# The order of every engine's work, written down as tables instead of planned

## The chip, the cores and the metric

The kernel runs on one core of one Trainium2 chip. The metric is the time of one execution in microseconds (us), as the median of several runs. Names of engines: PE is the matrix engine (TensorE), DVE the vector engine, ACT the scalar engine, POOL is GpSimd, and SP only issues transfers (DMAs) here.

## The reference

Two stages. First a gated linear attention, a recurrence over 768 positions for 4 batches and 8 heads of size 48:

```python
for t in range(S):
    state = alpha[:, :, t, :, None] * state + np.einsum('bhd,bhe->bhde', k[:, :, t], v[:, :, t])
    y[:, :, t] = np.einsum('bhd,bhde->bhe', q[:, :, t], state)
```

Its output, laid out as 3072 tokens of 384 values, goes through two layers of a feed-forward network with a squared relu between them:

```python
h = x @ w_in            # 3072 x 384 times 384 x 2048
r = np.maximum(h, 0.0)
g = r * r
return (g @ w_out).astype(np.float32)
```

## The kernel before, in words

The tokens are cut into 12 groups of 256 positions (`g` 0 to 11: three time blocks of four batches each). The recurrence is turned into matrix products within a group: decays are summed as logarithms by a triangular matrix product, a score product is masked, and a state of 48 x 48 per head is carried from one time block of a batch to the next. Then each group runs through the two layers.

The program is a list of operations, each added with a name, the engine or engines that may run it (`alts`), a cost, a priority, and what it reads and writes. For group `g` the names are:

- loads on SP or POOL: `lda`, `ldk`, `ldq`, `ldv` with the group's number (alpha, k, q, v; 384 KB each). Groups rotate over 4 buffers `raw`. A load of group 5 or later also waits for an operation of the group before: alpha for `ln`, k for `ekm`, q and v for `tr0`; and lda waits for the ldq of the group before it. `lda3` waits for `wout0`.
- weights on POOL: `win0`, `win1` (first layer, each half serves four of the eight steps), `wout0`, `wout1` (second layer).
- decays: `pr` (product of two alphas), `ln` and `lm` (logarithms on ACT), `m1`, `m1i`, `m1s` (PE), `ei`, `ea`, `es`, `ec` (exponentials on ACT), `bk`, `aq`, `lb` (products and a difference on DVE or POOL). For group 0 they come in two halves by heads: `ln0_0`, `ln1_0` and so on.
- `ekm`, `eqm` (scaled keys and queries, DVE), `tr` (transposes: on PE with an eviction `et` for groups 0 to 2, as transposing DMAs `tr0`, `tr1` on SP from group 3), `vc` (v cast to bf16), `p` (scores, PE), `mk` (mask, DVE), `kv` (state update alone), `y` (the output of the group; from group 2 on it also updates the state for the next), `sa`, `sc`, `sd` (the state's steps on DVE or POOL), `xe` (eviction), `xt` (transposed output: PE for groups 0 to 3, a DMA on SP from group 4), `xv`.
- layers: `s1_g_u` for u = 0 to 7 (6 matmuls into one of two banks of PSUM), `re` (relu, which frees the bank), `sq` (square of one or two relu tiles), `s2_g_j_s` (4 matmuls each; all of one j add up in the single bank `psO`), `oe` (eviction, which frees that bank), `out` (store, from two buffers `osb`). The last tile's second layer is `s2_11_1_0` and `s2_11_1_1` in other banks.
- set-up: constants without a name (`c1` and so on), and `table`, an explicit load of ACT's function table with logarithm and exponential (lines 480 to 486).

Before it emits anything, the kernel plans: `schedule` (line 159) replays the program with its costs. Whenever an engine is free, it takes from its ready operations the one of lowest priority. Where more than one engine is allowed, the operation goes to the one that would end it first, with a handicap for POOL (`BIAS`). A table `SHIFT` (line 49) moves the priority of some 360 names. The outcome is one fixed list per engine. On the chip each engine runs its list in order and waits at semaphores where an input is not there yet; nothing is chosen at run time. `fill` puts matmuls on zeros into PE's list where the plan has gaps before the first s1, `place` works out which waits are needed, `emit` writes the five lists.

Of the kernel before, what the change touches and what calls it, by code (L numbers as in the profile page):

```python
# [1174 lines left out]
```

## Time and profile before

| | before |
|---|---|
| median of 3 runs | 174.81 us (174.69 to 175.29) |
| the profiled execution's own time | 176.21 us |
| its span (first to last instruction) | 174.5 us |
| PE busy | 169.1 us, 97% of the span |
| DVE, ACT, POOL busy | 121.3, 117.6, 18.8 us |
| granted clock of PE | 1.00 throughout |
| bytes moved by DMA | 33.36 MB, mean 191 GB/s |

A line of a timeline gives the start, the length, the engine, the line of the kernel, the operation, what it writes and reads, the shape, how many instructions were merged, and in brackets the idle time before it with what ended that. PEld is PE's weight load, which runs beside matmuls. Lines of the engine name "SPq" are issues of transfers; a transfer lands later.

### The profile page before, as it was taken

What the parts mean: (1) busy time and instruction counts of PE and PEld (TensorE: products, weight loads), DVE (VectorE), ACT (ScalarE), POOL (GpSimd) and SP (SyncE); (2) the same over time, 40 slices, a digit from 0 to 9 for tenths busy, and PEclk for the clock granted to TensorE, in tenths of its full rate; (3) what the DMA queues carried; (4) which work ended last, traced back from release to release, by engine and by line L of the source; (5) the groups of instructions that cost most, each with busy time, mean ns of one, the idle gap of its engine ahead of it and who ended that gap; (6) DMA issues with size and microseconds to landing.
All of it is one profiled execution on the core that took longest, in us unless ns stands there. A gap on an engine that the chain in (4) does not pass through costs nothing.

```text
span 174.5 us, 5094 instructions
## 1 busy us (share of the span) xinstructions
PE 169.1 (97%) x2237; PEld 130.5 (75%) x2237; DVE 121.3 (70%) x197; ACT 117.6 (67%) x211; POOL 18.8 (11%) x28
## 2 busy tenths in 40 slices
PE   7989999999999999999999999999999999999994
PEld 2556898856886697777788886778788697688773
DVE  5497799797967869866778966868849726322230
ACT  3848698868869569768768757378668564566440
POOL 3159010022102120000100000000200000000000
DMA  5999999979998999798998897999899690040022
GB/s 139 324 297 190 274 303 216 230 208 280 274 229 125 274 235 188 200 222 151 278 212 211 228 196 180 275 201 251 201 214 208 115 196 4 0 135 4 10 80 90
DMA packets 74743, 33.36 MB, mean 191 GB/s; under 512 B 71649, under 2 KB 71905, under 8 KB 74721
## 3 DMA queue, kind: packets, MB, share of 16 engines
q1 hardware_dynamic: 73184, 28.32, 71.4%
q0 software_dynamic: 1536, 4.72, 12.1%
q8 instruction: 17, 0.28, 0.7%
q14 instruction: 6, 0.04, 0.1%
HBM read 25.17 MB, written 4.72 MB: 171 GB/s over the span
## 4 chain that ended last, share of the span: by engine, by line
PE 56%; DMA 26%; ACT 6%; DVE 4%; SPq 3%; POOL 2%; issue 1%
PE psO L1089 22%; PE psWH L1042 22%; DMA raw<-in_v_dram 9%; DMA wout<-in_moe_w_out_dram 8%; DMA raw<-in_alpha_dram 5%; DMA raw<-in_q_dram 5%; SPq L568 3%; PE psO L1143 2%; POOL raw L568 2%; ACT rr L1050 2%; PE psX L843 2%; PE psX L1012 2%; ACT vbf L742 1%; PE psZ L811 1%; PE psX L832 1%; PE psX L940 1%
## 5 line engine op out<-in xcount | busy, mean ns | idle before, releaser
L1042 PE MATMUL psWH<-xt,win 128*128 128x256 bf16 x576 | 73.9, 275 | 0.5 <-ACT rr L1050 0.2
L1042 PEld LDWEIGHTS psWH<-xt,win 128*128 128x128 bf16 x576 | 65.0, 145 | 6.2 <-DVE rr L1052 1.6
L1089 PE MATMUL psO<-wout,gt 128*128 128x384 bf16 x368 | 68.9, 326 | 0.0
L1050 ACT ACTIVATE rr<-psWH 128x512 bf16<-128x512 f32 x83 | 48.9, 596 | 21.5 <-PE psWH L1042 20.0
L1089 PEld LDWEIGHTS psO<-wout,gt 128*128 128x128 bf16 x368 | 34.8, 98 | 18.3 <-DVE gt L1060 0.2
L1060 DVE TENSOR_TENSOR gt<-rr 128x1024 bf16<-128x1024 bf16 (+1 forms) x47 | 28.4, 608 | 25.1 <-ACT rr L1050 24.5
L951 DVE TENSOR_TENSOR pm<-psX,caus 128x1024 bf16<-128x1024 f32 x12 | 14.6, 1220 | 2.4 <-PE psZ L940 2.1
L951 DVE TENSOR_TENSOR pm<-psZ,caus 128x1024 bf16<-128x1024 f32 x12 | 14.6, 1216 | 1.5 <-PE psZ L940 1.4
L1097 ACT ACTIVATE osb<-psO 128x384 f32<-128x384 f32 x19 | 9.3, 489 | 6.8 <-PE psO L1089 6.3
L971 ACT ACTIVATE xbf<-psX 128x768 bf16<-128x768 f32 x12 | 9.7, 806 | 5.0 <-PE psX L832 4.1
L746 DVE TENSOR_TENSOR qks<-raw,eq 128x384 bf16<-128x384 f32 x18 | 10.3, 605 | 3.0 <-DMA raw<-in_q_dram 3.0
L1143 PE MATMUL psO<-zero 128*128 128x512 bf16 (+1 forms) x37 | 10.5, 417 | 1.3 <-DVE zero L489 1.3
L741 POOL CAST vbf<-raw 128x768 bf16<-128x768 f32 x4 | 3.7, 930 | 71.5 <-DMA raw<-in_v_dram 71.5
L1064 ACT ACTIVATE gt<-rr 128x512 bf16<-128x512 bf16 (+1 forms) x13 | 10.8, 828 | 0.4
L751 DVE TENSOR_TENSOR qks<-raw,ek 128x768 bf16<-128x768 f32 x11 | 10.7, 969 | 0.4 <-ACT ek L663 0.3
L1052 DVE TENSOR_SCALAR rr<-psWH 128x512 bf16<-128x512 f32 x13 | 8.9, 687 | 2.0 <-PE psWH L1042 1.6
L742 ACT ACTIVATE vbf<-raw 128x768 bf16<-128x768 f32 x7 | 5.9, 845 | 3.5 <-DMA raw<-in_v_dram 3.5
L717 ACT ACTIVATE la<-raw 128x384 f32<-128x384 f32 x8 | 4.2, 523 | 5.3 <-DMA raw<-in_alpha_dram 5.2
L1143 PEld LDWEIGHTS psO<-zero 128*128 128x128 bf16 x37 | 3.5, 108 | 4.6 <-issue 1.9
L906 DVE TENSOR_TENSOR smd<-psZ,sbd 128x384 bf16<-128x384 f32 x8 | 4.4, 554 | 3.4 <-PE psX L832 3.4
L675 DVE TENSOR_TENSOR prd<-raw 128x384 f32<-128x384 f32 x7 | 4.0, 569 | 2.9 <-DMA raw<-in_alpha_dram 2.9
L678 ACT ACTIVATE lab<-prd 128x384 bf16<-128x384 f32 x10 | 5.2, 520 | 1.1 <-POOL prd L677 0.6
(115 smaller groups left out, 165.9 us busy)
## 6 DMA issues: line engine op xcount, KB each, us to landing
raw<-in_alpha_dram SPq DMA_DIRECT2D x11, 384.0 KB, 4.2
raw<-in_k_dram SPq DMA_DIRECT2D x11, 384.0 KB, 5.1
raw<-in_q_dram SPq DMA_DIRECT2D x11, 384.0 KB, 4.2
raw<-in_v_dram SPq DMA_DIRECT2D x11, 384.0 KB, 4.8
out_dram<-osb SPq DMA_DIRECT2D x11, 384.0 KB, 4.3
win<-in_moe_w_in_dram POOLq DMA_DIRECT2D x2, 768.0 KB, 9.9
wout<-in_moe_w_out_dram POOLq DMA_DIRECT2D x2, 768.0 KB, 15.2
raw<-in_alpha_dram POOLq DMA_DIRECT2D x1, 384.0 KB, 9.7
```

Source lines behind the costliest of these rows:

```text
L746: add("dve", lambda e, j=j, dst=dst: e.tensor_tensor(dst, RAW[r][:, 2, :, j, :].rearrange("p (n x) d -> p n x d", x=2), EQ[la][:, j].rearr ...
L751: add("dve", lambda e, a=a, E=E: e.tensor_tensor(QKS[qs][:, a, :, :, 0:D], RAW[r][:, 1 + a].rearrange("p h j d -> p j h d"), E[la][:].rear ...
L951: add("dve", lambda e, hf=hf, psT=psT: e.tensor_tensor(PM[pm][:, hf].rearrange("p r n j t -> p (r n) (j t)"), psT[:, :, :].rearrange("p r ...
L971: add("act", lambda e: e.activation(XBF[x2][:], psX[:, :, 0:HD], AF.Copy), act_ns(2 * HD), p0 + 6100, reads=[("ps", "X", 0), ("ps", "X", 1 ...
L1042: ins = pe.matmul(psH[hb][:, i * T:(i + 1) * T], WIN[:, kk, hidden(fj)], mov, start=(kk == 0), stop=(kk == KT - 1))
L1050: add("act", lambda e, hb=hb, rr=rr: e.activation(rr, psH[hb], AF.Relu), act_ns(512), pu + 600, reads=[("ps", "H", hb)], writes=[("rr", rb ...
L1052: alts={"dve": (lambda e, hb=hb, rr=rr: e.tensor_scalar(rr, psH[hb], 0.0, None, ALU.max), dve_ns(512))})
L1060: add("dve", lambda e, dst=dst, sq=sq: e.tensor_tensor(dst, sq, sq, ALU.mult), 148 + k * 267, pu + 1200, reads=[("rr", rb, h) for h in ran ...
L1064: "act": (lambda e, dst=dst, sq=sq: e.activation(dst, sq, AF.Square), act_ns(k * 512))})
L1089: ins = pe.matmul(psS, GT[gt][:, fj, j, :], WOUT[:, fj, :], start=(fj * parts % FT == 0), stop=((fj + 1) * parts % FT == 0))
L1097: add("act", lambda e, j=j, psS=psS: e.activation(OSB[ob][:, j], psS, AF.Copy), act_ns(DM), ps_ + 700, reads=[keyS], writes=[("osb", ob, j ...
L1143: pr.fill(lambda n: lambda pe: pe.matmul(psO[:, 0:n], ZERO[:, 0:128], ZERO[:, 0:n], skip_group_check=True), ((512, 216, 420), (256, 109, 2 ...
```

## The change

The planner no longer chooses. For each engine a table `ORDERS` gives the names in the order in which that engine runs them; every operation is fixed to the engine in whose table it stands. `SHIFT`, `BIAS` and `AFFINITY` go. `schedule` still replays the program to get start times for `fill` and `place`, but takes the next operation from the table. One constant of that replay changes (`DMA_LAST` of POOL, 1900 to 1500). The operations themselves, their sizes, buffers and dependencies stay.

Against the lists of before: 45 operations go from ACT to DVE (30 of them `re`, 4 `xe`, 5 `et`), 33 from DVE to ACT (19 `sq`, 10 `re`), 22 from DVE and 6 from ACT to POOL (15 `sq`, 6 `bk`, 3 `vc`, 2 `sd`, `aq2`, `pr11`), and 5 from POOL to ACT or DVE (`vc5`, `vc7`, `vc10`, `pr3`, `sd2`).

The tables of POOL and SP in full, the others where the text speaks of them:

```diff
+ORDERS = {
+    "pe": """
+        m10_0 m11_0 tr00_0 tr10_0 kv0 p0_0 tr01_0 tr11_0 m11 p1_0 y0 xt0 tr0_1 tr1_1 s1_0_1 s1_0_0 p0_1 s1_0_2 m1i2
+        s1_0_3 kv1 s1_0_4 s1_0_5 y1 s1_0_6 s1_0_7 xt1 m1s2 s2_0_0_0 s1_1_0 s1_1_1 s2_0_0_1 s1_1_2 s1_1_3 tr1_2 tr0_2
+        s1_1_5 s1_1_4 p0_2 s2_0_0_2 s2_0_0_3 s1_1_6 m1i3 s1_1_7 s2_0_1_0 s2_0_1_1 kv2 s2_0_1_2 s2_0_1_3 m1s3 y2
...
+        s2_4_1_3 s1_5_5 s1_5_6 s2_5_0_0 s1_5_7 p0_7 s2_5_0_1 s2_5_0_2 s1_6_1 s1_6_0 s2_5_0_3 y7 s1_6_2 s2_5_1_0 m1i9
+        s1_6_3 s2_5_1_1 s1_6_4 s1_6_5 s2_5_1_2 s2_5_1_3 p0_8 s1_6_7 s2_6_0_0 s1_6_6 s2_6_0_1 s1_7_1 s1_7_0 s2_6_0_2
+        s1_7_3 y8 s1_7_2 s1_7_5 m1i10 s2_6_0_3 s1_7_4 s1_7_7 s2_6_1_0 s2_6_1_1 s2_6_1_2 s2_6_1_3 s1_7_6 p0_9 s2_7_0_0
+        s1_8_1 s2_7_0_1 s1_8_0 s1_8_3 s2_7_0_2 y9 s2_7_0_3 s1_8_2 m1i11 s1_8_5 s2_7_1_0 s2_7_1_1 s2_7_1_2 s1_8_4 p0_10
...
+        s2_10_0_1 s1_11_1 s2_10_0_2 s1_11_4 s1_11_3 s2_10_0_3 s1_11_6 s1_11_5 s2_10_1_0 s2_10_1_1 s2_10_1_2 s2_10_1_3
+        s1_11_7 s2_11_0_0 s2_11_0_1 s2_11_0_2 s2_11_0_3 s2_11_1_0 s2_11_1_1
+    """.split(),
+    "act": """
+        ln0_0 ln1_0 ei0_0 ei1_0 ea0_0 ea1_0 ec1_0 table ec0_0 c23 ln1 et11_0 vc1 ei1 ea1 xe0 et0_1 ec1 re0_0 ln2 ei2
...
+        vc8 re6_0 re6_1 oe5_0 ln9 lm9 re6_2 ei9 ea9 re6_4 sq6_3 oe5_1 es9 sq6_5 re6_6 re7_1 re7_0 lm10 ln10 re7_3 xe8
...
+        sq10_3 oe9_1 re10_7 re11_1 re11_3 oe10_0 sq11_6 oe10_1 sq11_5 oe11_0 oe11_10
+    """.split(),
+    "dve": """
+        c19 c8 c9 c10 c11 c12 c13 c16 c1 c17 c3 c18 c5 c6 ekm0_0 ekm1_0 eqm0_0 c7 et00_0 sa0 et10_0 eqm1_0 mk0_0
+        et01_0 c2 mk1_0 sc0 ekm1 eqm1 xv0 et1_1 re0_1 pr2 mk1_1 re0_2 mk0_1 sa1 sc1 re0_5 xe1 xv1 ekm2 eqm2 et1_2
...
+        re11_0 re11_2 sq10_7 re11_4 re11_6 re11_5 re11_7 sq11_7 oe11_11
+    """.split(),
+    "pool": """
+        c14 c15 c20 c21 c22 vc0 win0 lda2 win1 wout0 sd0 ldk2 ldq2 bk2 wout1 sq0_5 aq2 ldv2 sd1 sq0_6 sq0_7 bk3 vc3
+        pr5 sd3 vc4 bk5 sq2_5 sd4 pr6 bk6 sq3_6 vc6 sq5_6 sq6_1 vc9 sq7_3 bk10 sq7_1 pr11 bk11 sq8_3 sq8_5 sq8_6 sq9_3
+        sq11_1 sq11_3
+    """.split(),
+    "sp": """
+        lda0 ldk0 ldq0 ldv0 lda1 ldq1 ldv1 ldk1 lda3 ldq3 ldk3 ldv3 lda4 ldq4 ldk4 ldv4 lda5 tr1_3 tr0_3 ldk5 tr0_4
+        out0_1 tr1_4 ldq5 out1_1 ldv5 lda6 tr0_5 tr1_5 ldk6 ldq6 xt4 ldv6 lda7 ldk7 tr0_6 tr1_6 xt5 ldq7 out2_1 ldv7
+        out3_1 lda8 tr0_7 ldk8 tr1_7 ldq8 xt6 ldv8 lda9 tr0_8 ldk9 tr1_8 ldq9 xt7 ldv9 lda10 ldk10 tr0_9 out4_1 tr1_9
+        ldq10 xt8 ldv10 lda11 out5_1 ldk11 tr1_10 tr0_10 out6_1 xt9 ldq11 ldv11 tr1_11 tr0_11 out7_1 xt10 out8_1 xt11
+        out9_1 out10_1 out11_0 out11_10 out11_11
+    """.split(),
+}
...
-    BIAS = {"pool": 300}
-    DMA_LAST = {"sp": 800, "act": 800, "pool": 1900}
+    DMA_LAST = {"sp": 800, "act": 800, "pool": 1500}
...
-        op = Op(choices, prio + self.SHIFT.get(name, 0), name)
+        op = Op(choices, prio, name or f"c{len(self.ops)}")
...
+        place = {n: (e, k) for e, names in ORDERS.items() for k, n in enumerate(names)}
+        for op in self.ops:
+            e = place[op.name][0]
+            op.alts = {e: op.alts[e]}
...
-                while avail[e] and free[e] <= now + 1e-9:
-                    o = min(avail[e], key=lambda o: (o.prio, o.idx))
...
-                    avail[e].remove(o)
+                while len(order[e]) in avail[e] and free[e] <= now + 1e-9:
+                    o = avail[e].pop(len(order[e]))
```

For comparison, the lists that the planner of before gives POOL, and the start of ACT's and of PE's:

```text
pool: c14 c15 c20 c21 c22 vc0 win0 win1 sd0 lda2 ldk2 ldq2 ldv2 wout0 wout1 sd1 pr3 sd2 vc4 pr5 vc5 pr6 vc7 vc10
act:  table c23 ln0_0 ln1_0 ei0_0 ea0_0 ei1_0 ea1_0 ec1_0 ec0_0 et10_0 et01_0 ln1 et11_0 ei1 ea1 xe0 ec1 vc1 et1_1 re0_0
pe:   m10_0 m11_0 tr00_0 tr10_0 tr01_0 p0_0 kv0 tr11_0 p1_0 m11 y0 tr0_1 xt0 tr1_1 p0_1 s1_0_0 s1_0_1 kv1 s1_0_2 s1_0_3 y1 s1_0_4
sp:   ... lda8 ldk8 tr0_7 tr1_7 out4_1 xt6 ldq8 ldv8 lda9 ldk9 tr0_8 tr1_8 xt7 ldq9 ldv9 out5_1 lda10 ldk10 tr0_9 ...
```

More of the change, by code (lines that the diff above doesn't have):

```diff
@@ L12 @@
 LN_EXP_TABLE_SET = 6
+ORDERS = {
[3 more added lines that the diff above has]
+        s1_1_5 s1_1_4 p0_2 s2_0_0_2 s2_0_0_3 s1_1_6 m1i3 s1_1_7 s2_0_1_0 s2_0_1_1 kv2 s2_0_1_2 s2_0_1_3 m1s3 y2
+        s2_1_0_0 s2_1_0_1 xt2 m1i4 s2_1_0_2 s1_2_1 s2_1_0_3 s1_2_0 s1_2_3 s2_1_1_0 s2_1_1_1 s1_2_2 s1_2_5 m1i5 p0_3
+        s2_1_1_2 s2_1_1_3 s1_2_4 s1_2_7 y3 s1_2_6 s2_2_0_0 xt3 s2_2_0_1 s2_2_0_2 p0_4 s1_3_1 s1_3_0 s2_2_0_3 s1_3_3
+        s1_3_2 s2_2_1_0 s2_2_1_1 s2_2_1_2 y4 s1_3_4 s1_3_5 m1i6 s1_3_6 s2_2_1_3 p0_5 s1_3_7 s2_3_0_0 s2_3_0_1 s2_3_0_2
+        s2_3_0_3 s1_4_0 s1_4_1 s2_3_1_0 s1_4_2 y5 s1_4_3 s1_4_4 s2_3_1_1 m1i7 s2_3_1_2 s1_4_5 s2_3_1_3 s1_4_6 s1_4_7
+        p0_6 s2_4_0_0 s1_5_1 s1_5_0 s2_4_0_1 s2_4_0_2 s1_5_2 s1_5_3 s2_4_0_3 y6 s1_5_4 s2_4_1_0 s2_4_1_1 m1i8 s2_4_1_2
+        s2_4_1_3 s1_5_5 s1_5_6 s2_5_0_0 s1_5_7 p0_7 s2_5_0_1 s2_5_0_2 s1_6_1 s1_6_0 s2_5_0_3 y7 s1_6_2 s2_5_1_0 m1i9
+        s1_6_3 s2_5_1_1 s1_6_4 s1_6_5 s2_5_1_2 s2_5_1_3 p0_8 s1_6_7 s2_6_0_0 s1_6_6 s2_6_0_1 s1_7_1 s1_7_0 s2_6_0_2
+        s1_7_3 y8 s1_7_2 s1_7_5 m1i10 s2_6_0_3 s1_7_4 s1_7_7 s2_6_1_0 s2_6_1_1 s2_6_1_2 s2_6_1_3 s1_7_6 p0_9 s2_7_0_0
+        s1_8_1 s2_7_0_1 s1_8_0 s1_8_3 s2_7_0_2 y9 s2_7_0_3 s1_8_2 m1i11 s1_8_5 s2_7_1_0 s2_7_1_1 s2_7_1_2 s1_8_4 p0_10
+        s1_8_7 s1_8_6 s2_7_1_3 s1_9_1 s1_9_0 s2_8_0_0 s2_8_0_1 s2_8_0_2 s1_9_3 s2_8_0_3 s1_9_2 y10 s2_8_1_0 s2_8_1_1
+        s1_9_4 s1_9_5 s2_8_1_2 s2_8_1_3 s1_9_7 p0_11 s2_9_0_0 s1_9_6 s2_9_0_1 s1_10_1 s1_10_0 y11 s1_10_2 s2_9_0_2
+        s2_9_0_3 s1_10_3 s1_10_4 s2_9_1_0 s1_10_5 s1_10_6 s2_9_1_1 s2_9_1_2 s1_11_0 s2_9_1_3 s1_10_7 s1_11_2 s2_10_0_0
+        s2_10_0_1 s1_11_1 s2_10_0_2 s1_11_4 s1_11_3 s2_10_0_3 s1_11_6 s1_11_5 s2_10_1_0 s2_10_1_1 s2_10_1_2 s2_10_1_3
[3 more added lines that the diff above has]
+        ln0_0 ln1_0 ei0_0 ei1_0 ea0_0 ea1_0 ec1_0 table ec0_0 c23 ln1 et11_0 vc1 ei1 ea1 xe0 et0_1 ec1 re0_0 ln2 ei2
+        re0_3 sq0_1 ea2 re0_4 sq0_3 ec2 re0_6 re0_7 es2 re1_0 re1_1 sq1_1 re1_3 re1_2 sq1_3 re1_5 sq1_5 ln3 oe0_0 ei3
+        vc2 re1_6 ea3 ec3 sq1_6 oe0_1 es3 ln4 xe2 re1_7 ei4 ea4 lm4 ec4 re2_1 oe1_0 re2_0 es4 re2_3 ln5 re2_2 re2_5
+        sq2_3 ei5 lm5 ea5 re2_4 oe1_1 xe3 re2_7 xv3 ec5 sq2_6 es5 sq2_7 re3_1 re3_0 re3_3 vc5 re3_2 sq3_3 lm6 ln6
+        re3_4 sq3_1 ei6 ea6 oe2_1 ec6 re3_7 sq3_7 es6 oe3_0 re4_0 re4_1 xe5 ln7 re4_3 ei7 re4_5 oe3_1 lm7 ea7 re4_7
+        ec7 sq4_5 es7 re5_0 re5_1 sq4_6 vc7 re5_2 oe4_0 ln8 xe6 re5_4 ei8 lm8 ea8 re5_5 sq5_5 es8 re5_7 re5_6 sq5_7
+        vc8 re6_0 re6_1 oe5_0 ln9 lm9 re6_2 ei9 ea9 re6_4 sq6_3 oe5_1 es9 sq6_5 re6_6 re7_1 re7_0 lm10 ln10 re7_3 xe8
+        re7_2 ei10 oe6_0 re7_4 sq7_5 ea10 oe6_1 es10 re7_6 re8_1 vc10 sq7_6 re8_0 ln11 xe9 ei11 sq8_1 ea11 lm11 re8_5
+        re8_4 re8_7 sq8_7 oe7_1 es11 vc11 re9_0 oe8_0 oe8_1 re9_7 re9_6 re10_0 xe11 sq10_1 oe9_0 re10_3 re10_4 re10_6
+        sq10_3 oe9_1 re10_7 re11_1 re11_3 oe10_0 sq11_6 oe10_1 sq11_5 oe11_0 oe11_10
[3 more added lines that the diff above has]
+        et01_0 c2 mk1_0 sc0 ekm1 eqm1 xv0 et1_1 re0_1 pr2 mk1_1 re0_2 mk0_1 sa1 sc1 re0_5 xe1 xv1 ekm2 eqm2 et1_2
+        et0_2 c4 re1_4 pr3 mk1_2 mk0_2 ekm3 sa2 sc2 eqm1_3 pr4 aq3 eqm0_3 sd2 xv2 sq1_7 bk4 sa3 ekm4 lb4 eqm1_4 eqm0_4
+        sc3 mk0_3 mk1_3 sq2_1 sa4 re2_6 sc4 ekm5 lb5 eqm0_5 eqm1_5 oe2_0 mk1_4 mk0_4 sa5 xe4 sc5 re3_5 sq3_5 re3_6
+        ekm6 lb6 eqm1_6 eqm0_6 mk0_5 mk1_5 re4_2 pr7 sa6 sq4_1 re4_4 sc6 sq4_3 bk7 ekm7 sd5 re4_6 lb7 sq4_7 eqm1_7
+        eqm0_7 mk1_6 mk0_6 re5_3 sq5_1 pr8 sq5_3 sa7 sc7 bk8 oe4_1 ekm8 lb8 eqm1_8 eqm0_8 mk1_7 mk0_7 sd7 pr9 xe7
+        re6_3 sa8 bk9 lb9 re6_5 ekm9 re6_7 eqm0_9 eqm1_9 mk1_8 mk0_8 pr10 sq6_6 sq6_7 sa9 re7_5 re7_7 sd6 lb10 eqm1_10
+        ekm10 eqm0_10 mk1_9 mk0_9 re8_3 sq7_7 oe7_0 sa10 re8_2 lb11 ekm11 mk1_10 re8_6 eqm1_11 re9_1 eqm0_11 mk0_10
+        sq9_1 re9_3 re9_2 xe10 sa11 re9_5 re9_4 sq9_5 mk0_11 sq9_7 mk1_11 re10_1 sq9_6 re10_2 re10_5 sq10_5 sq10_6
+        re11_0 re11_2 sq10_7 re11_4 re11_6 re11_5 re11_7 sq11_7 oe11_11
[13 more added lines that the diff above has]
+}
@@ L42 @@
     SBUF_ONLY = ("pr", "bk", "aq", "ekm", "eqm", "sq", "sb", "sd")
-    BIAS = {"pool": 300}
-    DMA_LAST = {"sp": 800, "act": 800, "pool": 1900}
+    DMA_LAST = {"sp": 800, "act": 800, "pool": 1500}
     SWITCH = 95
     HALVED = {"qks": 3, "kqt": 3, "raw": 3, "ek": 3, "eq": 3, "acm": 2, "laf": 2}
-    AFFINITY = 2500
-    SHIFT = {
[55 rows of a table removed]
-    }
     def __init__(self, nc):
@@ L216, in schedule @@
                 push(0.0, "ready", op)
-        avail = {e: [] for e in engines}
+        avail = {e: {} for e in engines}
         order = {e: [] for e in engines}
@@ L231, in schedule @@
                 elif kind == "ready":
-                    best = None
-                    for e, (_, c) in op.alts.items():
-                        t = max(now, free[e]) + c + self.BIAS.get(e, 0)
-                        t += sum(o.alts[e][1] for o in avail[e] if (o.prio, o.idx) < (op.prio, op.idx))
-                        if best is None or t < best[0]:
-                            best = (t, e)
-                    avail[best[1]].append(op)
-            for e in engines:
-                while avail[e] and free[e] <= now + 1e-9:
-                    o = min(avail[e], key=lambda o: (o.prio, o.idx))
-                    if e == "pe" and o.mode[0] != mode:
-                        same = [x for x in avail[e] if x.mode[0] == mode and x.prio <= o.prio + self.AFFINITY]
-                        if same:
-                            o = min(same, key=lambda o: (o.prio, o.idx))
-                    avail[e].remove(o)
+                    e, k = place[op.name]
+                    avail[e][k] = op
+            for e in engines:
+                while len(order[e]) in avail[e] and free[e] <= now + 1e-9:
+                    o = avail[e].pop(len(order[e]))
                     o.eng = e
```

55 rows, old and new, of the table SHIFT are left out of this document.

## The prediction

> **What bounds the kernel now.** First the page's busy lines, to see whether one engine carries the span.
>
> ```profile
> PE 169.1 (97%) x2237; PEld 130.5 (75%) x2237; DVE 121.3 (70%) x197; ACT 117.6 (67%) x211; POOL 18.8 (11%) x28
> DMA  5999999979998999798998897999899690040022
> ```
>
> PE is busy from end to end, so what can be won is not other engines' work but holes in PE's stream. A busy PE can hide holes (a stalled matmul counts as busy), so I put the planner's order of operations beside the timeline of PE and compared starts. A first-layer step (`s1_g_u`, 6 matmuls) issues in 0.66 us, a second-layer step (`s2`, 4) in 0.65, `p` in 0.57, `y` with a state update in 1.05. From the first s1 (`s1_0_0`) at 18.46 to the last matmul group at 171.17 the stream lasts 152.7 us, and steps that lasted longer than their kind's usual time add up to only 2.3: 0.40 at s1_1_1, 0.12 behind m1i3, 0.14 at kv2 and 0.15 at m1s3 (0.81 before 41 us), 0.15 at m1i6, then 0.37 before y5, 0.25 before y7, 0.41 before s1_7_3 and 0.27 before s1_7_4 (1.30). So 2.3 us is all that a reordering behind 18.46 can return.
>
> What makes the late four holes? The timeline of PE (start, length, engine, line, what) and then that of ACT, around the largest:
>
> ```profile
> 114.34 0.88 PE L1042 MATMUL psWH<-xt,win 128*128 128x256 bf16 x6
> 115.41 0.88 PE L1042 MATMUL psWH<-xt,win 128*128 128x256 bf16 x6 [0.19 <-ACT rr L1050]
> ```
>
> ```profile
> 111.35 0.58 ACT L1050 ACTIVATE rr<-psWH 128x512 bf16<-128x512 f32 x1
> 114.34 0.53 ACT L717 ACTIVATE la<-raw 128x384 f32<-128x384 f32 x1 [2.42 <-DMA raw<-in_alpha_dram]
> 114.77 0.58 ACT L1050 ACTIVATE rr<-psWH 128x512 bf16<-128x512 f32 x1
> ```
>
> ACT's in-order queue holds `lm10`, a logarithm whose load lands at 114.3, ahead of `re7_1`, whose bank PE wants back. ACT idles 2.42 us and PE loses 0.41 + 0.27. The holes before y5 and y7 wait for `vc6` and `vc8` (73.31, 98.62), each started when its v load landed. The chain of waits over 83 to 100 us shows what the loads wait for:
>
> ```profile
> 84.31 4.31 DMA raw<-in_alpha_dram
> ...
> 89.76 0.70 ACT xbf L971
> ...
> 92.86 0.40 SPq L992
> 93.26 0.04 issue
> 93.31 0.58 SPq L568
> 93.89 0.04 issue
> 93.93 4.67 DMA raw<-in_v_dram
> 98.60 0.02 issue
> 98.62 0.85 ACT vbf L742
> ```
>
> Load, logarithm, transpose, then SP's queue, then the next load: a loop of one turn per group. The transpose issue tr0_7 starts at 86.82 and lands 6.2 us later behind two loads, tr0_8 starts at 98.78: 12.0 us a turn, against 12.5 of PE work per group (8 x 0.66 + 8 x 0.65 + p, y, m1i, switches). No slack worth the name: loads, not engine work, make the late holes.
>
> The last view is SP's waits and the head of the loads:
>
> ```profile
> SPq L568 <- DMA wout<-in_moe_w_out_dram: 21.4, 1, 21.4
> ```
>
> lda3, gated on wout0, waits until 30.42, because wout0 is the seventh of the eight POOL transfers (issued at 16.73).
>
> **The change part by part.** Which engine does what moves: by counting names, 28 operations come to POOL and 5 leave it, 45 go from ACT to DVE (30 of them relus), 33 from DVE to ACT. With the means of the rows (relu 0.60 ACT, 0.68 DVE; square 1.06 and 0.69; cast 0.84; reorder of a transpose 1.02 and 0.68) ACT loses about 5.6 us of its 117.6, DVE 2.3 of 121.3. Neither was the bound; beside PE this is worth nothing by itself.
>
> POOL's 28 are the new thing: 15 squares, 6 `bk`, 3 `vc`, 2 `sd`, `aq2`, `pr11`. No square ran on POOL before. Bounds: 0.69 us as on DVE; by its nearest row (`sd`, 384 elements, 0.83 us unhindered) 2.2 us for 1024 elements and 1.1 for 512. POOL is that row's engine, so I take 2.2 and 1.1: 10 x 2.2 + 5 x 1.1 + 13 x 0.85, less 5 x 0.95 = about 34 us more, 53 in all, which fits in 174. What it does to DVE is the question; here POOL's timeline and then DVE's:
>
> ```profile
> 7.93 0.82 POOL L613 CAST vbf<-raw 128x768 bf16<-128x768 f32 x1 [4.98 <-DMA raw<-in_v_dram]
> ```
>
> ```profile
> 7.95 1.21 DVE L620 TENSOR_TENSOR qks<-raw,ek 128x384 bf16<-128x384 f32 x1
> 9.09 0.55 DVE L620 TENSOR_TENSOR qks<-raw,eq 128x384 bf16<-128x384 f32 x1
> ```
>
> The same product takes 0.55 alone and 1.21 when it starts beside a POOL cast: it ends 0.41 after POOL does (8.75). So too the square at 22.56 (1.36 instead of 0.69) beside `sd1`. The Trainium skill ("SBUF — State Buffer", Who interferes with whom) says that a DVE instruction with two SBUF inputs and a GpSimd one that reads SBUF exclude each other, whichever starts first; these rows agree, and the rule speaks against this change. I take +0.2 for PE in the forecast, since most squares sit several PE steps ahead of their `s2`; bounds 0 and the rival's price below.
>
> Head: the new PE order starts s1_0_1 and s1_0_0 before p0_1. win0 lands at 17.9 (issue 9.37 + 8.5), so s1 cannot start before that; it starts 0.5 earlier and p0_1 (0.57) follows: nothing won. DVE now also does et10_0, et01_0 and two memsets (0.42 + 0.42 + 0.38) before xv0, which ended at 16.59 after 1.16 of idle gaps: 16.6 to 17.8, still under win0. But lda2 goes between win0 and win1. Loads in that queue land 1.1 to 1.9 apart (q2 25.8, v2 26.9), so win1 lands at some 22.9 instead of 21.6. By its steps PE reaches s1_0_4 at 17.95 + 4 x 0.72 + 0.57 + 0.27 + 0.45 = 22.1, with y1 (0.8) still to do, and waits 0.7. Part of it returns since m1i2 is already done: +0.4, bounds 0 and +0.85.
>
> wout0 moves ahead of ldk2, ldq2, wout1 and ldv2: a2, win1, wout0 land at about 19.1, 22.9 and 26.4 (3.5 us per weight half, from 26.9 to 30.4), so lda3 starts 4 us sooner. ldv2 now sits behind bk2, wout1, sq0_5 and aq2 on POOL; its issue comes at about 29 instead of 15.9 and lands by 34, while kv2 comes at 36 to 38: hidden, with 2 us to spare. Early holes are rearranged with this: of 0.81 I take half back, -0.4, bounds -0.81 and 0.
>
> Middle: SP's table puts one load ahead of tr0 where two stood (lda6 tr0_5, lda8 tr0_7, lda9 tr0_8), ldq ahead of xt, and stores later (out4_1 behind tr0_9, out5_1 behind lda11). A load's data take 1.2 us of the queue, so a turn of the loop falls from 12.0 to about 10.8, under PE's 12.5. ACT's table puts re7_1 and re7_0 ahead of lm10; vc6 moves to POOL. All four late holes have their cause moved: -1.30, bounds -1.30 and 0. The cost at out4_1: oe6_0 waits for it (two osb buffers), and stores took 1.5 to 6.2 us to land; between tr0_9 and the s2_6_1_0 that needs oe6_0 there are some 7 us of PE work, enough for the median of 3.7.
>
> Tail: after s2_10_1_3 come s1_11_7 and s2_11; sq11_5 (1.06 on ACT) sits behind oe10_1 but has 2 us before s2_11_0_2; sq11_7 has 1.95 us for 0.68 + 0.42. From 171.17 to the end nothing changes.
>
> Sum: -1.30 - 0.4 + 0.4 + 0.2 = -1.1. The profiled execution took 176.21 with a span of 174.5; the median of the runs is 174.81, 0.3 over the span. So a span near 173.4 and a median near 173.7.
>
> **Rivals.**
> The lock decides (slower). A relu ends at 144.16 (started 143.56) and its bank's next s1 starts at 144.67, 0.5 to spare, 0.43 for a DVE relu. Twenty more relus stand in DVE's queue, behind operations with two SBUF inputs that a POOL square can hold. Caught halfway, one is held 1.1 us, and PE loses 1.1 - 0.43 = 0.67, never regained. Two such collisions eat the gain; four among the ten wide squares give 173.7 + 2.7 = 176.4. For it: the rows above. Against: the square that was held 0.67 at 22.56 left no hole in PE's stream.
>
> The table load (about no change). `table` moves from the first place on ACT to behind two Ln and five Exp. The page of before has one ACT_TABLE_LOAD (1.28 us at 0.80, before the first data). If the first Ln and the first Exp each need a load there, up to 2 x 1.28 enter the path from lda0 (4.2) to ekm0_0; up to 0.6 of it hides under win0, and the s1 stream starts up to 1.5 late, of which the wait for win1 gives 0.7 back. +0.8 to +1.5: 174.7, between no change and slower. The Trainium skill ("ScalarE: Activation LUTs", Step-by-step) says a load is placed right before an activation whose set is not active; no run here shows that yet.
>
> Holes only move (no change): transfers in the new order take longer than before, or the loop is not shortened, since each load still waits for the transpose before it. Then -1.30 fails and the rest sums to +0.2: 175.0 at most, 174.8.
>
> **Chances and range.** Forecast 0.52, lock 0.26, table load 0.11, holes move 0.11. A measurement of this kernel tells 0.3% (0.5 us) from no change. Faster 0.52; same 0.16 (holes, half the table load); slower 0.32. Low end: both groups of holes gone at no cost, 174.81 - 2.1 = 172.7, less 0.1 for the hole at m1i6; high end 176.2, just under the lock's four collisions. Likeliest case alone: 172.6 to 174.2.
>
> **What would show it.** Right: lda3 issued near 26; no hole before y5, y7, s1_7_3, s1_7_4; ACT's idle before L717 under 1 us each; the first s1 near 18.0 with a wait before s1_0_4. Wrong: two or more ACT_TABLE_LOAD rows and a first s1 at 19 or later; POOL squares over 2.2 us with DVE L1060 or L746 rows doubled beside them and PE gaps released by DVE rr; PE holes that wait for in_alpha or in_v again, or for osb behind a late store.

## The result, and the profile after

The changed kernel takes 177.39 us (median; the kernel before 174.81), a ratio of 1.014 with a 95% interval of 1.0103 to 1.0177. On a second chip it took 177.38 against 174.88, 1.0145 (1.0102 to 1.0189). So it is 2.5 us slower, where 1.1 us less was forecast. Ratios leave out executions more than 1.5% above the fastest of their kernel; in the kernel with the table load first, below, some of those are the work of a hole of its own, so its ratio is a little too kind.

The profiled execution took 177.39 us with a span of 175.5. The page's busy line, its DMA row and the group of the new POOL squares:

```profile
PE 168.0 (96%) x2237; PEld 130.7 (75%) x2239; DVE 120.6 (69%) x189; ACT 111.6 (64%) x198; POOL 53.1 (30%) x51
...
DMA  5999999989999999998999999999996682202022
...
L1055 POOL TENSOR_TENSOR gt<-rr 128x1024 bf16<-128x1024 bf16 (+1 forms) x15 | 24.7, 1647 | 59.2 <-ACT rr L1042 52.9
```

PE's busy time is 1.1 us less than before, and the kernel is slower: the loss is not in PE's stream but ahead of it. From the first s1 to the last matmul group PE takes 152.13 us (before 152.72, where p0_1 still stood ahead of the first s1), but the first s1 comes at 20.05 instead of 18.46. PE's rows of the first s1, before and after:

```profile
18.46 1.53 PE L1042 MATMUL psWH<-xt,win 128*128 128x256 bf16 x12
20.05 1.53 PE L1034 MATMUL psWH<-xt,win 128*128 128x256 bf16 x12
```

The head of ACT's timeline (start, length, what, idle time before) tells why, first before, then after:

```profile
0.80 1.28 ACT L483 ACT_TABLE_LOAD   x1 [0.80 <-PEq L1160]
...
4.33 0.94 ACT L584 ACTIVATE laf<-raw 128x384 bf16<-128x384 f32 x2 [0.93 <-DMA raw<-in_alpha_dram]
6.04 0.49 ACT L605 ACTIVATE ek<-psX 128x384 f32<-128x384 f32 x1 [0.78 <-PE psX L596]
```

```profile
4.30 1.28 ACT L576 ACT_TABLE_LOAD   x1 [4.30 <-DMA raw<-in_alpha_dram]
5.60 0.94 ACT L576 ACTIVATE laf<-raw 128x384 bf16<-128x384 f32 x2
6.55 1.28 ACT L597 ACT_TABLE_LOAD   x1
7.84 0.87 ACT L597 ACTIVATE ek<-psX 128x384 f32<-128x384 f32 x2
...
9.69 1.28 ACT L475 ACT_TABLE_LOAD   x1
```

Three table loads where before had one, at 0.80, under the wait for the first data. Without a table chosen by hand the first logarithm gets a load, the first exponential another, and the third is `table` in its new place. The first hides nowhere: it starts only when a0 has landed (4.30), although ACT had idled 4.30 us. The second stands behind the logarithms. ln0_0 starts 1.27 us later than before, ei0_0 1.80; that is less than 2 x 1.28, since before ACT waited 0.78 for PE ahead of ei0_0.

The predicted effects in the middle are there. SP's wait for wout0 is shorter (21.4 before), and lda3 is issued at 26.73:

```profile
SPq L560 <- DMA wout<-in_moe_w_out_dram: 17.6, 1, 17.6
```

PE around s1_7_3 (109.63 is s1_7_1 and s1_7_0, 111.59 is s1_7_3), and lm10 on ACT:

```profile
109.63 1.47 PE L1034 MATMUL psWH<-xt,win 128*128 128x256 bf16 x12
110.94 0.81 PE L1081 MATMUL psO<-wout,gt 128*128 128x384 bf16 x4
111.59 0.82 PE L1034 MATMUL psWH<-xt,win 128*128 128x256 bf16 x6
```

```profile
111.63 0.52 ACT L709 ACTIVATE la<-raw 128x384 f32<-128x384 f32 x1
```

No idle time before lm10, no hole at s1_7_3 or s1_7_4 nor before y7. But the hole before y5 has grown from 0.37 to 1.05 us. PE, DVE and POOL there:

```profile
76.04 0.19 PE L824 MATMUL psX<-sbd,kqt 64*128 64x48 bf16 x1 [0.89 <-DVE pm L943]
```

```profile
69.65 1.78 DVE L743 TENSOR_TENSOR qks<-raw,ek 128x768 bf16<-128x768 f32 x1 [0.31 <-POOL ek L694]
...
71.82 1.90 DVE L738 TENSOR_TENSOR qks<-raw,eq 128x384 bf16<-128x384 f32 x2
73.64 1.21 DVE L943 TENSOR_TENSOR pm<-psX,caus 128x1024 bf16<-128x1024 f32 x1
```

```profile
69.58 1.04 POOL L1055 TENSOR_TENSOR gt<-rr 128x512 bf16<-128x512 bf16 x1
72.48 0.82 POOL L733 CAST vbf<-raw 128x768 bf16<-128x768 f32 x1 [1.87 <-DMA raw<-in_v_dram]
```

ekm6 takes 1.78 us instead of 0.95 beside the square sq3_6, and eqm0_6 (the second of the pair at 71.82) 1.23 instead of 0.55 beside vc6; mask and y5 follow late. So two suspects stand: the table load, and collisions of POOL and DVE. A third question is why the end of three of the late holes brought so little.

### The profile page after: what moved, and what is told of

Same layout as the page of the kernel before. It is cut to its first block, busy times and chain, and to the rows that moved or that the text cites. A ratio compares the mean times of both kernels' runs of the same rounds, so it can differ in the third digit from the quotient of the medians.

```text
span 175.5 us, 5118 instructions
## 1 busy us (share of the span) xinstructions
PE 168.0 (96%) x2237; PEld 130.7 (75%) x2239; DVE 120.6 (69%) x189; ACT 111.6 (64%) x198; POOL 53.1 (30%) x51
## 3 DMA queue, kind: packets, MB, share of 16 engines
q0 software_dynamic: 1536, 4.72, 12.2%
## 4 chain that ended last, share of the span: by engine, by line
PE 85%; DVE 6%; ACT 4%; DMA 2%; issue 1%; POOL 1%; DVEq 0%; ACTq 0%
PE psWH L1034 35%; PE psO L1081 33%; DVE qks L743 2%; PE psZ L803 2%; PE psX L835 2%; PE psX L932 2%; DMA raw<-in_alpha_dram 2%; PE psX L824 2%; PE psO L1135 2%; PE psX L1004 2%; PE psZ L932 1%; DVE pm L943 1%; PE psWH L676 1%; PE psZ L766 1%; POOL ek L694 1%
## 5 line engine op out<-in xcount | busy, mean ns | idle before, releaser
L1042 ACT ACTIVATE rr<-psWH 128x512 bf16<-128x512 f32 x63 | 37.0, 594 | 22.8 <-PE psWH L1034 22.2
L1055 POOL TENSOR_TENSOR gt<-rr 128x1024 bf16<-128x1024 bf16 (+1 forms) x15 | 24.7, 1647 | 59.2 <-ACT rr L1042 52.9
L1044 DVE TENSOR_SCALAR rr<-psWH 128x512 bf16<-128x512 f32 x33 | 22.6, 688 | 20.4 <-PE psWH L1034 20.3
L1056 ACT ACTIVATE gt<-rr 128x1024 bf16<-128x1024 bf16 (+1 forms) x26 | 23.6, 906 | 1.5 <-DVE rr L1044 1.2
L738 DVE TENSOR_TENSOR qks<-raw,eq 128x384 bf16<-128x384 f32 x18 | 12.0, 678 | 2.6 <-DMA raw<-in_q_dram 1.4
L743 DVE TENSOR_TENSOR qks<-raw,ek 128x768 bf16<-128x768 f32 x11 | 11.8, 1076 | 1.4 <-POOL ek L694 1.4
L694 POOL TENSOR_TENSOR ek<-ek,raw 128x384 f32<-128x384 f32 x6 | 6.3, 1052 | 15.9 <-ACT ek L687 15.9
L1052 DVE TENSOR_TENSOR gt<-rr 128x512 bf16<-128x512 bf16 (+1 forms) x19 | 10.5, 562 | 0.1
L963 ACT ACTIVATE xbf<-psX 128x768 bf16<-128x768 f32 x8 | 6.5, 807 | 4.7 <-PE psX L824 3.7
L669 POOL TENSOR_TENSOR prd<-raw 128x384 f32<-128x384 f32 x3 | 3.5, 1162 | 14.0 <-DMA raw<-in_alpha_dram 14.0
L687 ACT ACTIVATE ek<-psWH 128x384 f32<-128x384 f32 x10 | 4.9, 490 | 3.9 <-PE psWH L679 2.3
```

The source lines that it names most:

```text
L738: add("dve", lambda e, j=j, dst=dst: e.tensor_tensor(dst, RAW[r][:, 2, :, j, :].rearrange("p (n x) d -> p n x d", x=2), EQ[la][:, j].rearr ...
L743: add("dve", lambda e, a=a, E=E: e.tensor_tensor(QKS[qs][:, a, :, :, 0:D], RAW[r][:, 1 + a].rearrange("p h j d -> p j h d"), E[la][:].rear ...
L1042: add("act", lambda e, hb=hb, rr=rr: e.activation(rr, psH[hb], AF.Relu), act_ns(512), pu + 600, reads=[("ps", "H", hb)], writes=[("rr", rb ...
L1044: alts={"dve": (lambda e, hb=hb, rr=rr: e.tensor_scalar(rr, psH[hb], 0.0, None, ALU.max), dve_ns(512))})
L1052: add("dve", lambda e, dst=dst, sq=sq: e.tensor_tensor(dst, sq, sq, ALU.mult), 148 + k * 267, pu + 1200, reads=[("rr", rb, h) for h in ran ...
L1055: alts={"pool": (lambda e, dst=dst, sq=sq: e.tensor_tensor(dst, sq, sq, ALU.mult), 200 + k * 840), "act": (lambda e, dst=dst, sq=sq: e.act ...
```

## Experiments on the table load

**The kernel before, once more.** No edit.

> The kernel before, unchanged, for a second profile of it. Its profiled execution on record took 176.21 us, 1.4 over the median of its runs (174.81), so the trace that the prediction worked from may hold stalls that the usual execution lacks. Theory A (the late holes of the matrix engine, 1.30 us behind loads, are part of every execution): the holes before y5, y7, s1_7_3 and s1_7_4 are there again, with the same releasers, and the span is 174.5. Theory B (they belong to that one execution): most of the 1.3 us is gone, the span is near 173.1 and the time near 174.8.

176.05 us, span 174.3. Its holes are not those of the first profile: 0.72 before m1i3, 1.48 before p0_3 (waiting for a transposing DMA), 0.13 before y5, 0.29 before y7, none at s1_7_3 and s1_7_4. The first s1 comes at 17.84, not 18.46. Both profiled executions of this kernel (176.21 and 176.05) lie above all but three of the 23 times taken beside the second (174.4 to 175.7 for most). What a trace of it shows behind transfers is one draw.

**Only the table load moved, in the kernel before.**

```diff
     pr.schedule()
+    act = pr.order["act"]
+    t = act.pop(0)
+    k = next(i for i, o in enumerate(act) if o.name == "ec0_0")
+    t.start = t.end = act[k].start - 1
+    act.insert(k, t)
...
```

> The kernel before with only its table load moved to the place that the change gives it, behind ec1_0; all else stays. Theory table load: four ACT_TABLE_LOAD rows (the copy c23, the first Ln, the first Exp, the explicit one), two of them on the path to ekm0_0; the first s1 at 20.0 to 20.6 instead of 18.46 and the time 174.8 + 1.6 to 2.1 = 176.4 to 176.9. Theory lock: under 0.6 slower, 175.4 at most, since win0 hides it.

177.07 us, ratio 1.0117 (1.0081 to 1.0154): 2.0 us lost by this edit alone, nearly the whole loss. The profile has four table loads (one for c23 at 0.79, then at 4.24, 6.49 and 9.90), a first s1 at 20.82, and 0.59 us of holes in all. The start comes 2.4 to 3.0 us later, the end 2.0, because transfers get a head start and PE waits less for them. Here the load at 9.90 lies on the path too, since et10_0 stands behind it on ACT; in the changed kernel only the first two do.

**The changed kernel with `table` first.**

```diff
-        ln0_0 ln1_0 ei0_0 ei1_0 ea0_0 ea1_0 ec1_0 table ec0_0
+        table ln0_0 ln1_0 ei0_0 ei1_0 ea0_0 ea1_0 ec1_0 ec0_0
```

> The changed kernel with one name moved: table stands first on ACT again. Theory table load (three loads of 1.28 us where one was, two of them between the landing of lda0 and ekm0_0): one ACT_TABLE_LOAD row, the first s1 at 17.9 to 18.2 instead of 20.05, the time 177.4 - 2.0 = 175.4, at most 0.7 of it lost again to a wait for win1 (176.1). Theory lock (POOL's new work holds DVE, the table load hides under win0): the first s1 moves by less than 0.6 and the time stays over 176.8.

One load, the first s1 at 17.86, as expected; but the median is 177.29, ratio 1.0076 (1.0038 to 1.0114). The times fall in groups: four at 175.27 to 175.55, six at 176.8 to 178.0, two at 179.5 and 179.75. The profile is of the last group. The timelines of DVE, POOL and PE in it:

```profile
27.21 1.81 DVE L743 TENSOR_TENSOR qks<-raw,ek 128x768 bf16<-128x768 f32 x1 [0.19 <-DMA raw<-in_k_dram]
28.94 3.83 DVE L743 TENSOR_TENSOR qks<-raw,eq 128x768 bf16<-128x768 f32 x1
```

```profile
27.20 1.01 POOL L703 TENSOR_TENSOR eq<-eq,raw 128x384 f32<-128x384 f32 x1 [0.61 <-ACT eq L701]
28.15 0.95 POOL L560 DMA_DIRECT2D raw<-in_v_dram  x1
29.11 0.84 POOL L907 TENSOR_TENSOR sbd<-tmp,acm 128x384 bf16<-128x384 f32 x1
29.91 2.03 POOL L1055 TENSOR_TENSOR gt<-rr 128x512 bf16<-128x512 bf16 x2
```

```profile
32.83 1.41 PE L766 MATMUL psZ<-ident,qks 128*128 128x128 bf16 x14 [2.26 <-DVE qks L743]
```

eqm2 takes 3.83 us instead of 0.96. By these rows it started 0.17 us before sd1 on POOL and yet ended 0.83 after the last of three POOL operations that ran one behind the other (sd1, sq0_6, sq0_7). The three took their usual time. In the changed kernel's own two profiles eqm2 just escaped: it ended at 31.93 when sd1 started at 31.85. The windows of this execution (length, then busy time of PE, PEld, DVE, ACT, POOL with counts, then granted clock) show what followed on PE:

```profile
30.00:32.00 2.00, 0.57 (x6) 0.33 (x4) 2.00 (x1) 1.70 (x4) 1.94 (x2) 1.00 1.03 270
32.00:34.00 2.00, 1.17 (x14) 1.18 (x15) 1.14 (x2) 0.78 (x1) 0.00 (x0) 0.79 1.11 363
34.00:36.00 2.00, 2.00 (x14) 1.64 (x12) 1.09 (x3) 0.23 (x1) 0.00 (x0) 0.50 1.14 313
36.00:38.00 2.00, 2.00 (x41) 1.34 (x40) 1.10 (x3) 0.68 (x2) 0.00 (x0) 0.86 0.70 178
```

Behind the hole of 2.4 us PE is granted half its clock until about 36.6: (0.21 + 0.50 + 0.14) x 2 = 1.7 us of clock on top. Together 4.1, the distance of 179.5 from the fastest group. No profile fell into the group near 177; that it comes from eqm2 too is what a later run has to show.

## Experiments on the collisions

**Table first, and the group at y5 off POOL.**

```diff
 pool: ... pr6 -bk6 -sq3_6 -vc6 sq5_6 ...
 dve:  ... re3_6 +bk6 ekm6 +sq3_6 lb6 ...
 act:  ... re4_1 +vc6 xe5 ...
```

> The kernel of e1 with three operations taken off POOL: bk6 and sq3_6 go back to DVE, vc6 to ACT behind re4_1. In the changed kernel bk6 (1.29 on POOL), the hold of ekm6 by sq3_6 (1.78 instead of 0.95) and of eqm0_6 by vc6 (1.23 instead of 0.55) end in a hole of 1.05 us before y5. Theory lock: the hole shrinks to 0.4 or less and the time falls 0.6 to 1.0 under e1. Theory table load alone: no more than 0.2 under e1, since PE catches up at a later wait anyway.

The hole before y5 is 0.37 instead of 1.02. Median 175.91, ratio 1.0045 (1.0013 to 1.0076); the fast group (174.96 to 176.07) is where it was, a group at 177.03 to 178.04 is still there, and one time of 179.40.

**And aq2, sd1, sq0_6, sq0_7 on DVE.**

```diff
 pool: ... sq0_5 -aq2 ldv2 -sd1 -sq0_6 -sq0_7 bk3 ...
 dve:  ... xe1 +sd1 xv1 ekm2 +aq2 eqm2 +sq0_6 +sq0_7 et1_2 ...
```

> The kernel with the table load first and bk6, sq3_6, vc6 off POOL, and now also aq2, sd1, sq0_6 and sq0_7 on DVE. Theory 1 (lock): the times of 177 us that the two kernels with the table load first still showed come from eqm2, which took 3.83 us in a profile because sd1, sq0_6 and sq0_7 ran on POOL one behind the other; with them on DVE, eqm2 takes 0.96, no hole before tr1_2, no time near 177 us, median 175.0 (174.5 to 175.5). Theory 2 (order of the loads): what is late is k2 itself, issued behind wout0; ekm2 still starts at 27 or later, a hole of about 1 us before tr1_2 stays, the times stay in two groups, median near 176.

Median 175.44, ratio 1.0005 (0.9983 to 1.0026). No group near 177: all but one of its times (178.88) lie between 174.94 and 176.52. eqm2 in DVE's timeline:

```profile
29.46 0.96 DVE L742 TENSOR_TENSOR qks<-raw,eq 128x768 bf16<-128x768 f32 x1
```

POOL issues ldk2 and ldq2 where it did, so their place was not the cause; the run of POOL operations was. This repaired kernel is the changed order without the late table load and without these collisions. Here it can't be told from the kernel before; measured again, below, it is 0.4% slower. In its profile PE waits 0.70 before s1_0_4 for win1.

**The changed kernel's late table, the same seven operations off POOL.** The edits of the last two on the changed kernel.

> The changed kernel with its own ACT table (table load in its late place), but the seven operations of the run before off POOL. With the other kernels this makes a table of two by two. If the late table load is a loss of its own: first s1 near 20, time 1.3 to 1.9 us over the kernel with the table load first and the same POOL order, 176.3 to 176.9. If the collisions on POOL were all of the loss: within 0.5 us of that kernel, 175.0 to 175.5.

177.48, ratio 1.0118 (1.0084 to 1.0151), 2.04 over the repaired kernel beside it: the table load. Against the changed kernel nothing is won. y5 waits 0.68 less, but m1i9 now waits 1.12. POOL and DVE ahead of it:

```profile
100.93 1.89 POOL L1054 TENSOR_TENSOR gt<-rr 128x1024 bf16<-128x1024 bf16 x1 [2.22 <-ACT rr L1041]
```

```profile
101.03 2.20 DVE L666 TENSOR_TENSOR prd<-raw 128x384 f32<-128x384 f32 x1 [1.06 <-DMA raw<-in_alpha_dram]
```

pr9, the product for m1i9, starts when a9 has landed, 0.10 behind the square sq6_1 on POOL. It takes 2.20 us instead of 0.55 and ends 0.41 after the square. At its usual length it and the logarithm behind it (0.53) would have ended near 102.1, and PE came to m1i9 at 102.7: the whole hole is a collision that the seven moves left in. The changed kernel's own two profiles don't have it.

**The changed kernel, the last kernel and the repaired kernel on one chip.**

> The changed kernel unchanged, a second chip and a second profile. If the ratio belongs to the kernels and not to a chip: 1.012 to 1.016. The hole before y5 tells whether that collision stands in every execution (1.05 in the first profile, 0.46 with half loads): if it wanders, another size or none.

> The changed kernel with the seven operations off POOL, beside the changed kernel on one chip. If the collisions are a standing loss in the changed kernel: 0.7 to 1.0 us below it. If they are met in few of its executions, or what is won is waited off at a later load: 0 to 0.4 us below it.

> The same with the table load first, on the same chip. If the table load is the main loss: 1.8 to 2.2 us under the run before, and no difference that can be told from the kernel before (ratio 0.998 to 1.003).

Changed 177.38, 1.0145 (1.0102 to 1.0189); seven operations off POOL 178.06, 1.0159 (1.0114 to 1.0204); and table first 175.81, 1.0042 (1.0013 to 1.0070). The table load is 2.25 us by the last two. Taking the seven operations off POOL again wins nothing; the profile of that kernel has pr9 held again (2.02 us) and m1i9 1.13 late, and that hole is part of the 2.25. What collisions cost in all stays open, since no version with the late table load is free of them. The changed kernel's second profile has 0.38 before y5 instead of 1.05: vc6 started 0.4 later, behind a later v6, and touched eqm0_6 less. So that collision does not stand in every execution.

**Three more collisions removed.** sq7_1, sq7_3, sq8_3, sq8_5 to DVE, and

```diff
 pool: ... sq6_1 -vc9 ...
 act:  ... re6_4 +vc9 sq6_3 ...
```

> The first kernel of these four, with vc9 on ACT and sq7_1, sq7_3, sq8_3 and sq8_5 on DVE as well. In the profile those held eqm0_9, eqm1_10 and ekm11 for 0.5 to 0.9 us each and left no hole on PE. If a collision only costs where the held operation has no slack: within 0.3 us of the first kernel. If each costs a part: 0.5 us less or more. This is also the candidate to beat both kernels: 174.3 to 175.0.

179.53, 1.0199 (1.0152 to 1.0246): no test of collisions, since the place for vc9 was wrong. ACT's timeline:

```profile
106.77 0.84 ACT L734 ACTIVATE vbf<-raw 128x768 bf16<-128x768 f32 x1 [3.19 <-DMA raw<-in_v_dram]
```

ACT stands 3.19 us before vc9's load, a square and an eviction queue behind it, PE loses 2.93 and then again runs at half clock. On POOL the same cast waits with little behind it: there it is better placed.

## Experiments on the loads

**SP's new order and lm10's new place, in the kernel before.** The lists of before as tables, then:

```diff
 sp:  the changed kernel's table
 act: ... re7_0 -lm10 re7_1 +lm10 ln10 ...
```

> The kernel before, its orders written down as tables, with the changed kernel's order on SP and lm10 moved behind re7_1 on ACT; nothing else. If the four late holes of the prediction are a standing loss of 1.30 us: 173.4 to 174.0. If such holes belong to single executions (the second profile of the kernel before had none at s1_7_3 and s1_7_4, and one of 1.48 elsewhere): 174.6 to 175.4, no difference that can be told, with holes that wait for loads at other places.

185.85, 1.0606 (1.0571 to 1.0641). Where the other engines keep their old lists, out4_1 behind tr0_9 is a trap. The chain of waits:

```profile
112.22 1.75 SPq L753
...
114.02 2.81 DMA out_dram<-osb
...
116.86 0.50 ACT osb L1088
...
117.40 2.74 PE psO L1080 x8
```

oe6_0 waits for the store, s2_6_1_0 for oe6_0: 7.47 us of PE. That says nothing about the four holes, but something about tables: one engine's list can't be judged without the others.

**Half the loads, kernel before, on two chips.**

```diff
+            hh = 8 if g < 4 else 4
-            src = t[b, :, t0:t0 + T, :]...
+            src = t[b, 0:hh, t0:t0 + T, :]...
-            dst, key = RAW[r][:, j], ("raw", r, j)
+            dst, key = RAW[r][:, j, 0:hh], ("raw", r, j)
```

> The kernel before, in which the loads of groups 4 to 11 bring only the first four of eight heads (left out: the other half of those loads; the rest of each buffer keeps an earlier group's numbers), all engine work unchanged. It prices what loads cost the kernel before in its usual execution. If the prediction's term holds (1.30 us of late holes behind loads, standing): 1.2 to 2 us less than before, 173.2 to 174.0. If the median execution has hardly any of them: 0.5 us less at most, 174.5 or more.

> The kernel before with the loads of groups 4 to 11 halved (left out: the other half of those loads), on another chip. If loads cost the kernel before a standing 1.2 us: 0.993 of it again, 173.7 where the kernel before takes 174.9. If that cost belongs to some chips and executions: the time stays near 174.9 whatever the chip, so 0.998 to 1.001 where the kernel before takes 174.9.

174.93 against 176.19, 0.9934 (0.9904 to 0.9965); and 174.49 against 175.51, 0.9946 (0.9919 to 0.9972). Half of those loads cost the kernel before 1.0 to 1.3 us, on both chips. Left are 0.59 and 0.91 us of holes.

**Half the loads, changed and repaired kernel.** The same edit.

> The changed kernel with the same halves left out. With its first s1 2 us later its loads have a head start, so loads should cost it less than the kernel before: 0.5 us or less, 176.8 to 177.4, with the hole of about 1 us before y5 in place (a collision on POOL, not a load). If loads are what eats its gains: 1 us less or more, 176.4 or lower.

> The run before with the loads of groups 4 to 11 halved (left out: the other half of those loads). If loads eat what the new order wins: 1.2 us or more below the run before, near the kernel before with half loads (0.993 of the kernel before). If its own waits (win1 behind lda2, relu before s1_1_0, y5) eat it: 0.5 us below or less, 0.997 of the kernel before or more, with those holes in the profile.

Changed: 177.12 (176.64 to 177.72), 1.0054 (1.0029 to 1.0080). That is 0.3 less than with full loads, but on a chip where the kernel before takes 176.19; by the ratios (1.014) it would be 1.5 less. With full loads the changed kernel didn't run on that chip, so what loads cost it stays open. Its two profiles with full loads show no hole of note that a load ends.

Repaired: 175.04, 1.0010 (0.9989 to 1.0032), 0.77 less than with full loads on that chip (1.0042; the two intervals overlap a little). So loads take back some 0.8 us there, and even with half of them gone the new order is not as fast as the old one with half of them gone (0.993, 0.995). Its profile says why: first s1 to last group takes 151.79 us, against 150.74 and 151.18, with p0_1 (0.76 up to the next s1) now inside that stretch, while the first s1 starts no earlier (18.67, against 18.52 and 18.60). Standing holes add up to 1.08: 0.37 before y5, 0.39 before s1_1_0, 0.19 behind p0_1 (part of the 0.76), 0.13 before kv1.

## Experiments on a faster version

**win1 before lda2, repaired kernel,** then **v loads on POOL on top of it.**

```diff
 pool: ... win0 -lda2 win1 +lda2 wout0 ...
```

> The kernel with the table load first and seven operations off POOL (175.44, no different from before), with win1 issued before lda2 on POOL as the kernel before has it. The prediction gave 0.4 us (bounds 0 and 0.85) to this place, and the profile of that kernel shows a hole of 0.70 before s1_0_4 that ends with win1's landing. If that hole stands in every execution: 0.4 to 0.7 us less, 174.7 to 175.0. If the loads of the middle take back what PE wins at the head: within 0.2 us, 175.2 to 175.6.

```diff
 sp:   -ldv6 ... -ldv11
 pool: ... sd4 +ldv6 pr6 +ldv7 +ldv8 sq5_6 +ldv9 ... vc9 +ldv10 ... pr11 +ldv11 ...
```

> The run before with ldv6 to ldv11 issued from POOL instead of SP's queue, so that a turn of load, logarithm, transpose, load is one load (about 1.2 us) shorter. If the load loop is the bound that takes back what other edits win: 0.5 to 1.5 us less than the run before, 173.5 to 174.7, faster than both kernels. If not: no change, or slower where the issue on POOL (0.95 us each) holds a DVE operation: 175 to 176.

180.51, 1.0219 (1.0162 to 1.0275), and 192.47, 1.0861 (1.0788 to 1.0935). In the first, PE waits 3.01 us for m1i2, which stands early in its new list, and then runs at half clock. The chain of waits, from lda2's issue to m1i2:

```profile
11.84 10.75 DMA raw<-in_alpha_dram
...
23.77 0.34 PE psWH L675
```

lda2 ahead of win1 is what the new PE list needs; the wait for win1 is its price. In the second the load loop was not tested: each ldv waits on POOL for a transpose, with POOL's work queued behind it. POOL's timeline:

```profile
69.40 0.92 POOL L560 DMA_DIRECT2D raw<-in_v_dram  x1 [7.37 <-DMA kqt<-qks]
70.33 1.01 POOL L669 TENSOR_TENSOR prd<-raw 128x384 f32<-128x384 f32 x1
```

pr6 comes at 70.33 and PE waits 1.78 for m1i6, with half the granted clock behind that hole as well. PE's row of m1i6, and the windows behind it:

```profile
71.95 0.34 PE L676 MATMUL psWH<-lab,linc 128*128 128x384 bf16 x1 [1.62 <-ACT lab L670]
```

```profile
73.00:74.00 1.00, 1.00 (x7) 0.49 (x5) 0.75 (x3) 0.97 (x3) 0.00 (x0) 0.71 1.12 402
74.00:75.00 1.00, 1.00 (x30) 0.71 (x32) 0.97 (x3) 0.79 (x3) 0.00 (x0) 0.50 1.43 179
```

**win0 sooner, kernel before.**

```diff
-    AFTER = {..., ("win", 0): (1, "a"), ...
+    AFTER = {..., ("win", 0): (0, "v"), ...
 pe: ... tr1_1 -p0_1 s1_0_0 s1_0_1 +p0_1 kv1 ...
```

> The kernel before with win0 issued once v0 has landed instead of a1 (about 0.6 us sooner), and p0_1 behind s1_0_1 instead of ahead of s1_0_0; a candidate to beat both kernels. If win0's landing sets the start of the s1 stream: first s1 at 17.0 to 17.5 instead of 17.8 to 18.5, 0.3 to 0.6 us less. If what is won at the head is waited off at loads, or win0 only shares the bandwidth with the loads of group 1: no difference that can be told.

175.90 against 175.51, 1.0022 (0.9993 to 1.0052): no difference. The first s1 comes at 17.72, straight behind the zero matmuls of `fill` that PE's list holds there, so this doesn't tell when win0 landed; and kv1 then waits 1.40, because p0_1 came later. None of these versions beats the kernel before.

## Why the prediction was wrong

**The step that failed most is the head.** The forecast had the first s1 near 18.0, under cover of win0; it came at 20.05 and 19.91. The mechanism was named as a rival, at 0.11 and with +0.8 to +1.5. Both were too low. Alone it costs 2.0 us (1.0117), and 2.04 and 2.25 between kernels that differ in nothing else (pr9's hole, of 1.12 and 1.13, may be part of both). The price counted "up to 0.6" as hidden under win0 and 0.7 as returned at win1. With the table load first, PE goes into the first s1 at 17.86 without a wait for win0 (17.85 in a second kernel; only a third profile has such a wait, 0.65), and the changed kernel has no wait before s1_0_4 that a late start could fill. What enters is not the full 2 x 1.28 = 2.56 either: between the changed kernel and the one with the table load first, ei0_0 comes 1.80 later (7.84 against 6.04, where ACT waits 0.89 for PE), then ekm0_0 on DVE runs beside vc0 on POOL (0.95 instead of 0.57), and the first s1 is 2.19 late. The chance was the larger error: the text had the move of `table`, the single load of before and the skill's rule, and nothing stood against it. By that rule (the Trainium skill, "ScalarE: Activation LUTs", Step-by-step) a load stands right before an activation whose set isn't active; the traces at 4.30 and 6.55 agree.

A smaller step of the head failed too: the first s1 was to start 0.5 earlier, so that p0_1 behind it costs nothing. In the profiles of the repaired order it starts at 17.85 to 18.67, in those of the kernel before at 17.84 to 18.60, so the 0.76 of p0_1 comes on top. That fits the repaired kernel's small loss; no run moves p0_1 alone in it.

**The starting point was mixed.** The sum took 1.1 us off the span of the profiled execution (174.5) and then added the 0.3 that lie between that span and the median of other executions. From the execution's own time the same sum gives 176.21 - 1.1 = 175.1. The holes that were subtracted are part of why that execution took 1.4 us more than the median, and the second profile of the same kernel has others.

**The late holes, -1.30.** The size was near: half of the loads cost the kernel before 1.0 to 1.3 us. (The holes before y5 and y7 were put some 0.1 too high each: the step ahead of y4, y6 and y8 takes 0.75 as well, and nothing waits there.) That the new order takes this cost away is not what the runs show. Three of the four holes are gone in both profiles of the changed kernel, and that before y5 stands (1.05 and 0.38) and ends with the mask on DVE. But that kernel starts 2 us later, and a late start alone empties the kernel before of all four (0.59 of holes left with the table late). The repaired order, which starts as early as before, still pays some 0.8 for its loads. The rival that holes only move was right here. The turn of the loop did become shorter, from 12.7 and 12.5 to 12.2 and 11.8 us in two profiles each (a fifth of the time from the issue of lda6 to that of lda11), less than the 1.2 forecast. The DMA row, at 9 tenths in nearly every slice up to about 140 us, suggests that the engines of the DMA are nearly as full as PE; that was only read, not tested apart.

**The early holes, -0.4.** Nothing was won: the repaired kernel has 0.73 of holes before 41 us in one profile (0.19, 0.13, 0.41) and 1.4 in the other, before had 0.81. The wait before s1_0_4 was foreseen at 0.7; it is 0.70 in one profile of the repaired kernel, none in the other, and none in the changed kernel, which starts later.

**The lock, +0.2.** Its sum for this kernel stays open: in the two profiles the collision at y5 costs about 0.7 and next to nothing, and the version without it ran into another. The operations that were held were the products ekm, eqm and pr9, and PE waited behind them, not for relus as the rival had it. Its price, 0.67 for one, fits y5, is low for pr9 (1.12 and 1.13), and missed the case of several POOL operations in a row: 2.4 us of PE, and 1.7 of clock. That case was met only once the table load was out of the way (groups at 177 and 179.5, gone with four operations moved).

**Right:** lda3's issue (near 26: 26.73), the squares (2.2 and 1.1: 1.89 to 2.21 and 1.03 to 1.05), POOL's 53 us (53.1), the end of the holes at y7, s1_7_3 and s1_7_4, no hole at out4_1, and the tail. Added up: the repaired order +0.1 to +0.7 by its two measurements, the table load 2.0 to 2.25, in all 2.1 to 2.95; measured 2.5.
